# Exchanged halves of two weight matrices: VectorE copies between partition halves, or TensorE products with a permutation

## The chip, the cores and the metric

The kernel runs on one core of a Trainium2 chip. The metric is the device time of one execution in microseconds (us), the median of several executions. TensorE (PE in the profile; PEld is its weight load) multiplies, VectorE (DVE), ScalarE (ACT) and GpSimd (POOL) work on elements, SyncE (SP) issues transfers. Each engine works through its own queue in order and waits for others by semaphores.

## The reference

Attention over pooled queries, and then a multiplicative feed-forward block on its output:

```python
# q, k, v: (8 batches, 8 heads, 1152, 64)
q_pool = q.reshape(B, H, S // 2, 2, D).mean(axis=3)          # 576 queries
scores = scale * np.matmul(q_pool, k.transpose(0, 1, 3, 2))
attn = softmax(scores)
x = np.matmul(attn, v) -> (4608 tokens, 512)                 # heads side by side
a = x @ w1        # (512, 1024)
b = x @ w2        # (512, 1024)
h = a * b @ w3    # (1024, 1024)
out = h @ w_out   # (1024, 512)
```

Inputs and output are single precision; the kernel computes in half precision with single-precision sums.

## The kernel before

**Attention.** Two heads of one batch make a pair, one in partitions 0 to 63, the other in 64 to 127; there are 32 pairs, counted from 0. A pair's scores are 9 key blocks of 576 columns, cut through all pairs into 324 chunks of 512 columns. `scores` (L294) makes one chunk for both heads with products of half height, 64 rows each, so that the two heads' products run at the same time in two halves of the array (tile `psc`, two buffers). `expo` (L300) takes the exponential of both at once on ScalarE, into `er`. When a pair's chunks are done, two bursts (`attend`, L312 and L321, full-height products, tile `po`) multiply by the values; VectorE normalizes them (L340, L343, L354), and transposes on SP's queue (L348) put the result into `xT`, the left side of the feed-forward block.

**Keys and queries** of later pairs are turned by TensorE (`prep_pe`, tile `t`, L262; evicted by VectorE at L252 and L256), from pair 9 on by transposes on SP's queue (L166, L172).

**Feed-forward.** w3 and w_out are multiplied with each other once (`T16`; products `pT`, L477, evicted at L472, after transposes `w3t`, L465), so that each batch needs its gate products (`pg`, L514: x times w1 and x times w2, multiplied by VectorE at L497 and L506) and its output products (`pp`, L535). These products, too, are of half height: block `ft` of half h runs in rows 64h to 64h+63. Of a feature block m, the rows that half h needs lie in one partition half of the weights as they are loaded, and for the other m in the opposite one. So w1 and w2 are kept twice: `w1sb[:, 0]` as loaded, `w1sb[:, 1]` with partitions 0 to 63 and 64 to 127 exchanged. The gate products read `[(m + h) % 2]`:

```python
    nc.tensor.matmul(t, (w1sb, w2sb)[w][s, (m + h) % 2, m // 2, fs], x(s, m), ...)   # L514
```

**The exchange.** The weights are loaded in two column halves of 512 by POOL's queue (`load_ffn`, L376: w1sb, then w2sb, first half then second). `swap_halves` (L383) multiplies one block of 128 rows by 512 columns by a permutation matrix `swap` (L391) into a PSUM bank `sw`, and VectorE (L397) or, for one block of four, ScalarE (L394) writes it as half precision into `[:, 1]`. That is 4 blocks for each of 2 matrices and 2 column halves: 16 products, 12 evictions on VectorE, 4 on ScalarE. POOL builds `swap` from the identity with two copies (L638, L639).

**The order** of all this is made by a planner in the kernel while it records. It keeps a clock for each of TensorE's two halves (`clock`), one for VectorE (`vec`), the end of each exp (`exp_done`) and the PSUM banks in hand (`spare`), adds a booked cost for each block, and chooses what is recorded next: a burst when one is due, the next chunk when its exp buffer is free, otherwise one product of the waiting work (`step`: first keys, queries and w3 turns, then feed-forward). `swap_due` allows a permutation product when the planner's clock has passed 47 (first column half) or 57 (second) and enough banks are free; it is asked after each burst and wherever `step` finds nothing. The gate products of a column half are let in when its last exchange is done (`copied`). What is recorded is the fixed order on each engine; nothing is chosen while the kernel runs. A change of a booked cost therefore moves the order of everything after it, on all queues.

Of the kernel before, what the change touches and what calls it, by code (L numbers as in the profile page):

```python
# [8 lines left out]
FP16 = mybir.dt.float16  # L9
# [14 lines left out]
def kernel(  # L24
# [11 lines left out]
    nc = tc.nc  # L36
# [4 lines left out]
    NC = dm // 128  # L41
# [4 lines left out]
    T_SC, T_EXP, T_SEM, T_PV, LEAD = 0.219, 1.03, 0.25, (1.65, 1.3), 2.6  # L46
    SCALE = 0.5 * float(D) ** -0.5

    const = ctx.enter_context(tc.tile_pool(name="const", bufs=1))
# [14 lines left out]
    vts = [const.tile([128, 2, NJ, VW], FP16, name=f"vt{i}") for i in range(4)]  # L64

    ident = const.tile([128, 128], FP16)
    swap = const.tile([128, 128], FP16)
    seen = const.tile([1, 2], FP16)
    handed = const.tile([1, 1], FP32)

# [8 lines left out]
    clock = [0.0, 0.0]  # L79
    vec = 0.0  # L80
    exp_done = []
    spare = [(0.0, n) for n in range(4)]

    def vector(n, at):

        nonlocal vec
        vec = max(vec, at + T_SEM) + 0.16 + n / 960
        return vec

    def bank(pre, n, dt=FP32):  # L90
        if n >= 4:
            return psum.tile([128, 2, 512], FP32, tag="psc", bufs=2, name=pre)[:, 0, :]
        return psum.tile([128, 2048 // (4 if dt == FP32 else 2)], dt, tag=f"ff{n}", bufs=1,
                         name=pre)

    def take():
        return spare.pop(0)[1]

    def give(n, t):
        spare.append((t, n))  # L100
        spare.sort()
# [196 lines left out]
    def expo(c):  # L298
        r = (c * CH) % RING
        nc.scalar.activation(out=er[:, :, r:r + CH], in_=psc.pop(c), func=AF.Exp,  # L300
                             bias=0.0, scale=SCALE)

    def attend(P, u):

        n = take()
        po = bank("po", n)
        for j in range(NJ):
            for i in range(4):  # L310
                r = ((P * NJ + j) * SQ) % RING + 128 * i
                nc.tensor.matmul(  # L312
                    po[:, VW * i:VW * i + D + 1], er[:, u, r:r + 128],
                    vts[P % 4][:, u, j, 0:D + 1],
                    start=(j == 0 and i == 0), stop=(j == NJ - 1 and i == 3),
                    skip_group_check=True)
        if u == 0:
            for j in range(NJ):
                r = ((P * NJ + j) * SQ) % RING + 512
                for s in range(2):  # L320
                    nc.tensor.matmul(  # L321
                        po[64 * s:64 * s + 64, 4 * VW:4 * VW + D + 1], er[:, s, r:r + 64],
                        vts[P % 4][:, s, j, 0:D + 1], start=False, stop=(j == NJ - 1),
                        skip_group_check=True)
        at = max(clock[0], clock[1], exp_done[last_chunk(P)] + T_SEM) + T_PV[u]
        clock[:] = [at] * 2
        give(n, normalize(P, u, po, 5 - u, at))
        b, hp = divmod(P, 4)
        if u == 0 and b % 2 == 1:
            nc.sync.dma_start_transpose(  # L330
                out=xR[:, hp, b // 2].rearrange("p u r -> p (u r)"),
                in_=rems[:, hp].rearrange("p s d -> p (s d)"))
        if u == 0 and hp == 3:
            ended.append((b, [vec + (8.0 if b < 2 else 6.5)]))
# [29 lines left out]
    def load_w3(i):  # L364
        w3h.append(ffp.tile([128, 2, dff], FP16, tag="g", bufs=4, name="w3h"))
        nc.gpsimd.dma_start(
            out=w3h[i],
            in_=moe_w3.rearrange("(c p) f -> p c f", p=128)[:, 2 * i:2 * i + 2])
# [4 lines left out]
    def load_ffn(h):  # L373
        cols = slice(512 * h, 512 * h + 512)
        for dst, src in ((w1sb, moe_w1), (w2sb, moe_w2)):
            nc.gpsimd.dma_start(out=dst[:, 0, :, cols],  # L376
                                in_=src.rearrange("(c p) f -> p c f", p=128)[:, :, cols])
            swaps[h].extend((dst, c, cols) for c in range(NC))

    swaps = ([], [])  # L380
    copied = [[1e9], [1e9]]

    def swap_halves():  # L383

        half = 0 if swaps[0] else 1
        dst, c, cols = swaps[half].pop(0)
        n = take()
        t = bank("sw", n)  # L390
        nc.tensor.matmul(t, swap, dst[:, 0, c, cols], start=True, stop=True)  # L391
        clock[:] = [max(clock) + 0.22] * 2
        if c % 3 == 1:
            nc.scalar.copy(out=dst[:, 1, c, cols], in_=t)  # L394
            done = exp_done[-1] = max(exp_done[-1], clock[0] + T_SEM) + 0.6
        else:
            nc.vector.tensor_copy(out=dst[:, 1, c, cols], in_=t)  # L397
            done = vector(512, clock[0])
        give(n, done)
        if not swaps[half]:  # L400
            copied[half][0] = done + T_SEM

    def swap_due():
        half = 0 if swaps[0] else 1
        free = 3 if prep[0] or prep[1] else 2
        return bool(swaps[half]) and max(clock) > WEIGHTS[half] and len(spare) >= free and (
            spare[0][0] < min(clock))

    w3T = {}

# [26 lines left out]
    prep, ffn = ([], []), ([], [])  # L437
# [164 lines left out]
    def last_rows(places, lhsT):  # L602
# [24 lines left out]
        out=ident, in_=ident, compare_op=ALU.not_equal, fill=1.0,  # L627
# [7 lines left out]
    load_w3(1)  # L635
    load(3)
    load_w3(2)
    nc.gpsimd.tensor_copy(out=swap[:, 0:64], in_=ident[:, 64:128])  # L638
    nc.gpsimd.tensor_copy(out=swap[:, 64:128], in_=ident[:, 0:64])  # L639
    staged, prepped = 1, 1  # L640
    rest = prep_first()

# [18 lines left out]
    WEIGHTS = (47.0, 57.0)  # L661
# [5 lines left out]
    def due(c):  # L667


        if bursts and (c + 1) * CH > bursts[0][1] * PAIR + RING:  # L670
            return 1e9
        P = ((c + 1) * CH - 1) // PAIR
        return max(exp_done[c - 2] if c > 1 else 0.0, kq_done.get(P, 0.0))

    c = 0
    fresh = False
    while c < NCHUNK or bursts or ffn[0] or ffn[1]:
        h = 0 if clock[0] <= clock[1] else 1
        if bursts and (c > bursts[0][0] or c == NCHUNK) and spare and spare[0][0] < clock[h] and (
                fresh or c > bursts[0][0] + 1 or c == NCHUNK):  # L680
            attend(*bursts.pop(0)[1:])
            fresh = False
            while swap_due():
                swap_halves()
            continue
        if c >= NCHUNK or due(c) > clock[h]:
            fresh = False
            if c >= NCHUNK and not tail and not bursts:
                tail = True
                spare += [(max(clock), 4), (max(clock), 5)]  # L690
            keep = 1 if prep[0] or prep[1] or bursts and c > bursts[0][0] - 1 else 0
            if not step(h):
                if swap_due():
                    clock[:] = [max(clock) + 0.1] * 2
                    swap_halves()
                    clock[:] = [clock[0] + 0.1] * 2
                else:
                    clock[h] += 0.02
            while ended and not early and not prep[0] and not prep[1]:
                b, ready = ended.pop(0)  # L700
                add_batch(b, ready)
            continue
        at = c * CH / PAIR
        scores(c, h)
        fresh = True
        for i in range(2):
            clock[i] += T_SC
        expo(c)
        exp_done.append(max(exp_done[-1] if c else 0.0, max(clock) + T_SEM) + T_EXP)
        if c == 0:  # L710
            prep_rest(rest)
        if jobs:
            n, job = jobs.pop(0)
            job()
            vector(n, 0.0)
        if staged < NPE and at >= STAGE.get(
                staged, staged - (0.95 if staged < 4 else 1.3)):
            prep_stage(staged)
            staged += 1
        while events and at >= events[0][0]:  # L720
            _, n, act = events.pop(0)
            act(n)
        todo = prepped < NP and at >= PREP.get(prepped, prepped - (
            0.65 if prepped < 4 else 0.9 if prepped < NPE else 1.9))
        if todo and prepped >= NPE:
            prep_dma(prepped)
            prepped += 1
        elif todo and prepped < staged and prepped in kcs:
            prep_pe(prepped)
            prepped += 1  # L730
        elif early and c >= early[0][0] and len(w3T) < 4:
            w3_transpose(early.pop(0)[1])
        while turns and at >= turns[0][0]:
            turns.pop(0)[1]()
        c += 1
    for emit, store, _, _ in last[:-1]:
        n = take()
        t = bank("pp", n)
# [34 lines left out]
```

## Time and profile before

| | |
|---|---|
| time, median of 3 runs | 421.24 us (420.91 to 422.11) |
| span of the profiled execution, first to last instruction | 423.3 us |
| TensorE products by the permutation (L391) | 16, from 64.7 to 94.0 us |
| their evictions on VectorE (L397) | 12, 681 to 693 ns each, 8.2 us |
| their evictions on ScalarE (L394) | 4, 580 to 593 ns each, 2.4 us |
| first gate product (L514) | 76.0 us |
| POOL copies that build the permutation (L638, L639) | 2, at 21.5 and 21.7 us, 0.25 us each |
| loads of w1sb, issued / time to landing | 36.6 and 46.4 us / 15.9 us |
| loads of w2sb, issued / time to landing | 38.0 and 47.6 us / 17 us |
| granted TensorE clock, mean | 0.995 |

Of the profiled execution only its span is known, not its device time as the runs measure it. A busy share is a mean over the span; the chain of work that ended last is followed back from the last instruction and says for each piece of time which engine and line the end waited for. Matmuls are pipelined: a product's own duration (some 0.2 to 0.4 us) is longer than the spacing at which products follow each other, so that work is counted by the spacing or by its share of the chain. Lines named L are lines of the kernel before.

### The profile page before, as it was taken

Reading aid. Unit: us, or ns where it says so; the run is one execution under the profiler, and the core shown is the slowest. Engines: PE = TensorE matmul, PEld = TensorE weight load, DVE = VectorE, ACT = ScalarE, POOL = GpSimd, SP = SyncE. Lnnn points to the kernel's source line nnn. Section 1 sums busy time; section 2 is a strip of 40 time slices with the busy share of each in tenths; the row PEclk is TensorE's granted clock in tenths of the full one; section 3 lists DMA queues with packets and bytes.
Section 4 is the critical chain, followed back from the end, with each engine's and each line's share of the span. In section 5 each row is a group of like instructions: output and inputs, shape, how many; then the busy total and the mean of one; then the engine's idle time right before and its main releaser. Section 6 shows DMA issues by size and latency. Waiting matters only on the chain.

```text
span 423.3 us, 17431 instructions
## 1 busy us (share of the span) xinstructions
PE 403.7 (95%) x7666; PEld 318.0 (75%) x7666; DVE 218.9 (52%) x596; ACT 331.1 (78%) x382; POOL 191.2 (45%) x209
## 2 busy tenths in 40 slices
PE   3799999998999999999999899999999999999996
PEld 1366665777768887888788786788878887888993
DVE  2266656875435653565365663356446644542540
ACT  3968888887788888888888788889888888834432
POOL 8233345860566576555655556665569300000000
PEclk9999999999899999999999999999999999999999
DMA  8999999999699999999999999999996215102004
GB/s 120 206 207 202 186 205 204 189 161 121 110 154 206 152 141 153 196 144 121 192 170 132 139 134 132 190 185 150 137 170 141 42 35 133 43 19 101 4 11 141
DMA packets 94219, 59.02 MB, mean 139 GB/s; under 512 B 64832, under 2 KB 84544, under 8 KB 94144
## 3 DMA queue, kind: packets, MB, share of 16 engines
q0 software_dynamic: 26528, 33.56, 50.7%
q1 hardware_dynamic: 67456, 24.22, 35.1%
q8 instruction: 60, 0.98, 1.0%
q10 hardware_dynamic: 160, 0.13, 0.1%
q14 instruction: 15, 0.12, 0.1%
HBM read 67.11 MB, written 9.44 MB: 181 GB/s over the span
## 4 chain that ended last, share of the span: by engine, by line
PE 93%; ACT 3%; issue 2%; DMA 1%; DVE 0%; POOL 0%; DVEq 0%; ACTq 0%; POOLq 0%
PE pg L514 30%; PE psc L294 19%; PE po L312 18%; PE pp L535 15%; PE pT L477 4%; PE po L321 3%; ACT er L300 3%; PE t L262 1%; PE sw L391 1%; DMA kst<-in_k_dram 1%; PE w3t L465 0%; PE pp L608 0%; PE tb L195 0%; POOL qst L108 0%; ACT kc L207 0%
## 5 line engine op out<-in xcount | busy, mean ns | idle before, releaser
L300 ACT ACTIVATE er<-psc 128x1024 f16<-128x1024 f32 x324 | 308.8, 1030 | 52.0 <-PE psc L294 48.7
L294 PE MATMUL psc<-qT,kT 64*128 64x384 f16 (+7 forms) x1152 | 132.3, 291 | 4.6 <-ACT er L300 3.8
L514 PE MATMUL pg<-xT,w2sb 64*128 64x256 f16 x1024 | 131.3, 270 | 0.0
L514 PE MATMUL pg<-xT,w1sb 64*128 64x256 f16 x1024 | 130.7, 271 | 0.1
L514 PEld LDWEIGHTS <-w1sb 64*128 64x128 f16 x1280 | 97.9, 94 | 10.9 <-issue 2.7
L514 PEld LDWEIGHTS <-w2sb 64*128 64x128 f16 x1280 | 96.7, 94 | 6.2 <-issue 0.4
L535 PE MATMUL pp<-T,gT 64*128 64x512 f16 (+1 forms) x552 | 94.4, 376 | 0.0
L312 PEld LDWEIGHTS <-er 128*128 128x128 f16 x2304 | 74.5, 98 | 17.6 <-issue 15.0
L294 PEld LDWEIGHTS <-kT 64*128 64x128 f16 x1152 | 60.6, 95 | 32.5 <-issue 16.8
L312 PE MATMUL po<-vt,er 128*128 128x65 f16 x2304 | 82.4, 194 | 2.0 <-issue 1.8
L506 DVE TENSOR_TENSOR gT<-pg,asb 128x256 f16<-128x256 f32 (+1 forms) x160 | 66.3, 417 | 20.8 <-ACT asb L494 16.3
L497 DVE COPY asb<-pg 128x256 f32<-128x256 f32 (+1 forms) x119 | 48.0, 404 | 32.1 <-PE pg L514 30.5
L340 DVE RECIPROCAL rz<-po 128x4 f32<-128x4 f32 x64 | 12.1, 189 | 89.7 <-PE po L312 46.0
L143 POOL TENSOR_TENSOR qp<-qst 64x1152 f16<-64x1152 f16 x23 | 54.5, 2370 | 1.0
L535 PEld LDWEIGHTS <-gT 64*128 64x128 f16 (+1 forms) x552 | 41.3, 94 | 13.8 <-issue 0.4
L168 POOL COPY seen<-kT 1x1 f16<-1x1 f16 x19 | 3.4, 180 | 88.0 <-DMA kT<-kc 88.0
L152 POOL COPY vt<-vst 128x1152 f16<-128x1152 f16 x28 | 32.1, 1150 | 4.6 <-issue 3.9
L123 POOL DMA_DIRECT2D vst<-in_v_dram x32 | 23.3, 729 | 17.2 <-DMA kst<-in_k_dram 7.4
L116 POOL DMA_DIRECT2D kst<-in_k_dram x33 | 24.0, 729 | 11.7 <-issue 3.0
L343 DVE TENSOR_TENSOR xn<-po,rz 128x256 f16<-128x256 f32 x64 | 27.2, 424 | 2.2
L494 ACT COPY asb<-pg 128x256 f32<-128x256 f32 (+1 forms) x41 | 12.8, 332 | 19.4 <-PE pg L514 18.9
L161 POOL COPY kc<-kst 128x1152 f16<-128x1152 f16 x23 | 26.9, 1169 | 0.0
(62 smaller groups left out, 256.2 us busy)
## 6 DMA issues: line engine op xcount, KB each, us to landing
qst<-in_q_dram POOLq DMA_DIRECT2D x32, 288.0 KB, 6.0
vst<-in_v_dram POOLq DMA_DIRECT2D x32, 288.0 KB, 8.2
kst<-in_k_dram POOLq DMA_DIRECT2D x31, 288.0 KB, 5.4
out_dram<-osb SPq DMA_DIRECT2D x32, 256.0 KB, 3.2
w3h<-in_moe_w_dram POOLq DMA_DIRECT2D x4, 512.0 KB, 15.6
wosb<-in_moe_w_out_dram POOLq DMA_DIRECT2D x1, 1024.0 KB, 13.8
xT<-xn SPq DMA_TRANSPOSE x64, 5.8
w1sb<-in_moe_w_dram POOLq DMA_DIRECT2D x2, 512.0 KB, 15.9
```

The costliest lines, as they stand in the source:

```text
L116: nc.gpsimd.dma_start(out=kst[P][:, :, js[0]:js[1], :], in_=k[b, h0:h0 + 2].rearrange("u (p j) d -> p u j d", j=NJ)[:, :, js[0]:js[1], :])
L143: (eng or nc.vector).tensor_tensor(out=qps[pp][r].rearrange("p c u d -> p u c d"), in0=src[:, :, :, 0, :], in1=src[:, :, :, 1, :], op=ALU.add)
L152: (eng or nc.vector).tensor_copy(out=vts[P % 4][:, :, :, 0:D], in_=vst.pop(P))
L161: nc.gpsimd.tensor_copy(out=kc.rearrange("p j u d -> p u j d"), in_=kst.pop(P))
L294: nc.tensor.matmul(t[:, u, o:o + ln], kT[P][s, j, :], qv[s, f0:f0 + ln], start=True, stop=True)
L300: nc.scalar.activation(out=er[:, :, r:r + CH], in_=psc.pop(c), func=AF.Exp, bias=0.0, scale=SCALE)
L312: nc.tensor.matmul(po[:, VW * i:VW * i + D + 1], er[:, u, r:r + 128], vts[P % 4][:, u, j, 0:D + 1], start=(j == 0 and i == 0), stop=(j == ...
L343: nc.vector.tensor_tensor(out=xn, in0=acc[:, 0:4, 0:D], in1=rz[:, 0:4].to_broadcast([128, 4, D]), op=ALU.mult)
L497: nc.vector.tensor_copy(out=a, in_=t[:, 0:n])
L506: nc.vector.tensor_mul(out=g, in0=b, in1=a)
L514: nc.tensor.matmul(t[:, n * w:n * w + n], (w1sb, w2sb)[w][s, (m + h) % 2, m // 2, fs], x(s, m), start=start, stop=stop, skip_group_check=True)
L535: nc.tensor.matmul(t, gT[h][s, i, cs], T16[s, i, :], start=start, stop=stop, skip_group_check=True)
```

## The change

The permutation products, their evictions and the permutation are removed. `swap_halves` is now one VectorE copy from 64 partitions of `[:, 0]` to the other 64 partitions of `[:, 1]`, over all four row blocks of one column half: 64 x 4 x 512 elements, 8 copies in all (2 matrices, 2 directions, 2 column halves). The planner books 0.69 us on VectorE for each and nothing on TensorE or ScalarE, and takes no bank. One copy is recorded after a chunk of scores when no other VectorE job waits and the planner's clock has passed the same 47 or 57; the places where the old exchange was asked for are gone. ScalarE's line of exps has no other work in it before the last part of the kernel.

In the order of the instructions this puts the first four copies among pair 5's key and query evictions and the last four around pair 4's normalizations and pair 6's key and query evictions; the order is the same up to the first copy and differs in many places behind it. TensorE has 16 products and 16 weight loads fewer.

```diff
-    swap = const.tile([128, 128], FP16)
...
         for dst, src in ((w1sb, moe_w1), (w2sb, moe_w2)):
             nc.gpsimd.dma_start(out=dst[:, 0, :, cols],
                                 in_=src.rearrange("(c p) f -> p c f", p=128)[:, :, cols])
-            swaps[h].extend((dst, c, cols) for c in range(NC))
+            swaps[h].extend((dst, s, cols) for s in (0, 64))
...
-    def swap_halves():
-        half = 0 if swaps[0] else 1
-        dst, c, cols = swaps[half].pop(0)
-        n = take()
-        t = bank("sw", n)
-        nc.tensor.matmul(t, swap, dst[:, 0, c, cols], start=True, stop=True)
-        clock[:] = [max(clock) + 0.22] * 2
-        if c % 3 == 1:
-            nc.scalar.copy(out=dst[:, 1, c, cols], in_=t)
-            done = exp_done[-1] = max(exp_done[-1], clock[0] + T_SEM) + 0.6
-        else:
-            nc.vector.tensor_copy(out=dst[:, 1, c, cols], in_=t)
-            done = vector(512, clock[0])
-        give(n, done)
-        if not swaps[half]:
-            copied[half][0] = done + T_SEM
+    def swap_halves(half, dst, s, cols):
+        src = slice(64 - s, 128 - s)
+        nc.vector.tensor_copy(out=dst[s:s + 64, 1, :, cols], in_=dst[src, 0, :, cols])
+        vector(512, 0.0)
+        if not swaps[half]:
+            copied[half][0] = vec + T_SEM
 
-    def swap_due():
+    def swap_due(now):
         half = 0 if swaps[0] else 1
-        free = 3 if prep[0] or prep[1] else 2
-        return bool(swaps[half]) and max(clock) > WEIGHTS[half] and len(spare) >= free and (
-            spare[0][0] < min(clock))
+        if swaps[half] and now > WEIGHTS[half]:
+            swap_halves(half, *swaps[half].pop(0))
...
-    nc.gpsimd.tensor_copy(out=swap[:, 0:64], in_=ident[:, 64:128])
-    nc.gpsimd.tensor_copy(out=swap[:, 64:128], in_=ident[:, 0:64])
...
             attend(*bursts.pop(0)[1:])
             fresh = False
-            while swap_due():
-                swap_halves()
             continue
...
             if not step(h):
-                if swap_due():
-                    clock[:] = [max(clock) + 0.1] * 2
-                    swap_halves()
-                    clock[:] = [clock[0] + 0.1] * 2
-                else:
-                    clock[h] += 0.02
+                clock[h] += 0.02
...
             n, job = jobs.pop(0)
             job()
             vector(n, 0.0)
+        else:
+            swap_due(max(clock))
```

## The prediction

> **What bounds the kernel now.** I read the page first, for the busy shares and the chain of work that ended last.
>
> ```profile
> PE 403.7 (95%) x7666; PEld 318.0 (75%) x7666; DVE 218.9 (52%) x596; ACT 331.1 (78%) x382; POOL 191.2 (45%) x209
> ...
> PE 93%; ACT 3%; issue 2%; DMA 1%; DVE 0%; POOL 0%; DVEq 0%; ACTq 0%; POOLq 0%
> ```
>
> TensorE (PE) is on the chain for 93% of the span and VectorE (DVE) for 0%. So time taken off TensorE counts, unless it then waits for something else, and time put on VectorE counts only where TensorE must wait for it. Next I read the chain in the stretch from 60 to 77 us, where the exchange is made (start, us, what):
>
> ```profile
> by line: PE pT L477 26.1%; PE psc L294 25.2%; PE sw L391 18.8%; PE po L312 17.6%; PE po L321 4.8%; PE t L262 4.2%; PE pg L514 3.5%; issue 0.1%
> ...
> 64.80 0.32 PE sw L391
> 65.12 0.32 PE psc L294 x4
> ...
> 69.67 0.22 PE psc L294 x2
> 69.89 0.54 PE sw L391 x2
> 70.43 0.33 PE psc L294 x4
> ```
>
> The chain has no waits here: the permutation products (sw) lie on it whole, and the scores behind one take 0.32 us where others take 0.22. Third, ScalarE's timeline (start, us; the exps x4 stand in a row) shows how fast chunks of scores can follow each other:
>
> ```profile
> 56.72 3.77 ACT L300 ACTIVATE er<-psc 128x1024 f16<-128x1024 f32 x4 [0.25 <-PE psc L294]
> ```
>
> One exp lasts 1.02 us, four in a row 3.77, so they follow at (3.77 - 1.02) / 3 = 0.917 us. 324 of them need 297 us; the exps end near 371 us, so ScalarE has room.
>
> **The change, part by part.** *Removed from TensorE:* 16 products by the permutation. Eleven of them fill 18.8% of the 17 us above = 3.2 us, 0.29 each; 16 cost 4.7 us. About 0.3 us more goes with the slower scores behind them (0.10 each where no other full-height product is next to it, three places or so). Gross gain 5.0 us.
>
> *Given back.* TensorE's other work is the same but stands in another order: the first gate products (pg) come 210 score products into the order instead of 218, two chunks earlier, and the T products (pT) that the exchange used to alternate with are used up sooner. From the end of pair 3's second attend burst at 60.98 to the first gate product I added up the new order by the chain's pieces: ten chunks of scores 2.8, 27 T products 2.9, 27 transposes 0.8, two attend bursts 1.20 + 1.61: 9.3 us. Ten exps need 9.2, so there TensorE and ScalarE are even, and every unevenness is a wait. I walked both orders to the end this way: each product at its spacing in a run (T and output products 0.107 us, gate products 0.053, transposes 0.029, attend bursts 1.20 and 0.41, a permutation product 0.21), 0.10 at each change between half-height and full-height products, exps at least 0.917 apart, and a chunk's scores held until 0.25 us past the exp of two chunks before. TensorE waits 18.8 us in the old order (8 of them in the first 20 us) and 20.8 in the new one: 2.0 us are given back. At the same chunk the new order leads by 0.6 us (chunk 57), 1.6 (63), 2.3 (90), 2.9 (183) and 3.4 (240), and ends 3.0 earlier. With exps at 0.955 (what six at 96.75 us show), a hold of 0.15, or 0.05 to 0.15 per change, the end comes out 2.7 to 3.9 us earlier. I take 3.0.
>
> *Removed from ScalarE:* four evictions of 0.59 us, 2.4 us, in the walk. *Removed from VectorE:* 12 evictions, 8.2 us.
>
> *Added to VectorE:* 8 copies of 64 partitions x 2048 half-precision elements, SBUF to SBUF. No row copies between partition halves. The nearest are straight copies and evictions (count | busy us, mean ns | idle):
>
> ```profile
> L497 DVE COPY asb<-pg 128x256 f32<-128x256 f32 x103 | 43.5, 422 | 27.4 <-PE pg L514 25.8
> ...
> L397 DVE CAST w1sb<-sw 128x512 f16<-128x512 f32 x6 | 4.0, 687 | 0.6 <-PE sw L391 0.6
> ...
> L185 DVE COPY kc<-kst 128x1152 f16<-128x1152 f16 x6 | 2.7, 454 | 0.1
> ...
> L229 DVE COPY kc<-kst 128x768 f16<-128x768 f16 x1 | 0.3, 350 | 0.0
> ```
>
> The last two give 0.104 us per 384 elements, 0.271 ns each: 2048 elements cost 454 + 896 x 0.271 = 697 ns. The first two, out of PSUM, give 1.035 ns an element: at that pace a copy takes 687 + 1536 x 1.035 = 2.28 us. The low end is the first slope with no fixed part, 0.56 us. I take 0.70, because memory, type and kind of instruction are those of the L185 and L229 rows; only the partition offset is new. Eight cost 5.6 us, less than the 8.2 removed, but earlier and packed. VectorE (third of the engines' busy times) between 57 and 76 us:
>
> ```profile
> 57.00:76.00 19.00, 19.00 (x307) 11.14 (x304) 12.45 (x30) 16.53 (x19) 11.18 (x14) 1.00 1.21 203
> ```
>
> It is busy 12.45 of 19 us, with seven of the evictions (4.8 us) in it. With these out and eight copies in, it is 13.3: it fits. The tightest place is the first four copies, which stand in the order among pair 5's key and query evictions, right behind the normalization (xn) that ends at 56.97. Adding up 0.62 a copy (0.70 less the 0.08 by which neighbours overlap), two kT at 0.40, a T eviction 0.62, a handoff 0.12 and qT 0.38, qT is done at 61.4, against 58.7 now. Pair 5's scores begin in chunk 50, at 63.6 us: 2.2 us to spare. Behind qT the next normalization is some 0.5 us late, which delays a free PSUM bank and one transpose on SP, both with microseconds in hand (the chain shows no wait for either). If this cover is gone, every further microsecond lands on TensorE.
>
> *Waits.* The copies wait for the weights' DMAs. Where they stand, VectorE holds normalizations and evictions behind a copy that waits. POOL's own waits show the landings (last bracket: idle, who ended it):
>
> ```profile
> 52.70 0.60 POOL L108 DMA_DIRECT2D qst<-in_q_dram  x1 [2.69 <-DMA w1sb<-in_moe_w_dram]
> 55.38 0.72 POOL L123 DMA_DIRECT2D vst<-in_v_dram  x1 [2.09 <-DMA w2sb<-in_moe_w_dram]
> ...
> 65.36 0.60 POOL L108 DMA_DIRECT2D qst<-in_q_dram  x1 [1.73 <-DMA w2sb<-in_moe_w_dram]
> ```
>
> The first half is there by 55.4, its copies start at 57.0. In the second half w1sb was issued at 46.40 and takes 15.9, so 62.3, and its first copy comes near 64; w2sb is there by 65.3 and its copy stands behind pair 6's keys, near 68. No wait; 1.5 us to spare at the least. A weight landing 3 us late would hold VectorE for about 1.5.
>
> *POOL and SP:* two 0.25 us copies that built the permutation go; the load behind them waited for a DMA until 22.23 anyway: nothing. SP carries the same transposes and stores, with stores one or two places earlier or later; a store's issue takes 0.56 us (median), a transpose is 5.8 us on its way: at most half a microsecond of delay, under cover of the gate work that waits in line.
>
> *Against the change.* The row first: one straight VectorE copy (9.79 us, 0.45 long) ran while POOL issued a load at 9.98, and was no longer than the others (452 to 456 ns). [...]
>
> **The sum.** The profiled span is 423.3 us, 2.1 over the median 421.24 of the timed runs. Span: 423.3 - 5.0 + 2.0 = 420.3. The same 3.0 us off the median: 418.2. Own range by the walk 417.3 to 418.6, and 416.5 to 419.9 with half a pause (below) either way.
>
> **The rivals.**
>
> *Slow copies (slower than before).* If the crossing copy runs at the evictions' pace, it takes 2.28 us. The first four then end 4 x 1.58 = 6.3 us later; 2.2 are covered, so pair 5's scores stall about 4.1 us. The second four stand in what is left: VectorE's free 5.7 us in the stretch against 12.6 added in all, so about 2.8 more. 418.2 + 6.9 = 425.1; up to 427 if nothing is made up. It decides from about 0.70 + 2.2 / 4 = 1.25 us per copy, and the time is worse than before from 0.70 + (3.0 + 5.7) / 8 = 1.8. For it: no row of such a copy. Against it: same memories, type and instruction as the 454 ns row.
>
> *A pause moves.* TensorE stands still for "issue", for no semaphore, at 101.70, and at 105 its clock is halved (the chain's piece, then a row by time whose last columns are clock, DMA share, GB/s):
>
> ```profile
> 101.70 1.81 issue
> ```
>
> ```profile
> 105.00:106.00 1.00, 1.00 (x14) 0.73 (x10) 0.93 (x3) 1.00 (x2) 0.96 (x2) 0.50 0.00 0
> ```
>
> The clock is below 1 from 104.8 to 108.2, which costs 1.7 us: 3.5 in all. Others stand at 51.72 (0.61) and 240.60 (1.49). These places lie multiples of 256 TensorE instructions apart, and the page's row of the instruction queue has 60 packets of 16 KB for 15,332 instructions, which is one packet per 256: it looks like late code. The new program has 32 TensorE instructions fewer before all later places, so a packet's end falls elsewhere: without this pause 414.7, with one more 421.7. For it: two or three large pauses among 60 packets. Against: nothing shifts it one way.
>
> *TensorE thins out.* The gain is lost if the chunks from 61 to 71 us are paced by ScalarE and DVE answers rather than by products: 2.7 us more given back, 420.9, no change. For it: ten exps 9.2 against 9.3 us of products. Against: behind the first gate product a backlog lasts to the end, since 50 us of feed-forward work run after the last attend burst, and the walk already holds these waits. [...]
>
> **How the numbers follow.** Forecast (416.5 to 419.9) 0.52; slow copies 0.13; a pause fewer 0.08; a pause more or a thinned TensorE that ends within 0.3% 0.14; the same ending above that 0.13. 0.3% (1.26 us) is what a measurement of this kernel can tell from no change: 419.98 to 422.50. So faster 0.60, same 0.14, slower 0.26. The range leaves out about 1 in 10 at each end: 414.7 to 424.5.
>
> **What would show it.** sw is gone and w1sb<-w1sb copies stand at 0.65 to 0.75 us between 57 and 70; the first gate product starts at 70.5 to 72 us instead of 76.0; pair 5's scores show no wait for qT; the exps of the stretch follow at 0.92 to 1.0. Wrong if a copy lasts over 1.25 us, if VectorE waits for w1sb or w2sb landings, or if "issue" or a clock of 0.50 has grown or shrunk by over 1.5 us.

## The result, and the profile after

| | median | runs |
|---|---|---|
| before | 421.79 us (419.83 to 424.84) | 20 |
| changed | 423.99 us (421.03 to 428.20) | 20 |

The ratio changed / before is 1.0048, with an interval of 1.0026 to 1.0069: the change makes the kernel slower, by 2.2 us of the medians (the interval is 1.1 to 2.9 us). The runs of the changed kernel also spread more widely, over 7.2 us against 5.0.

One trap lies in the profiles themselves. The profiled execution of the changed kernel took 421.03 us, its fastest of 20, with a span of 419.0; so 2.0 us lie around the span. By the same 2.0 the profiled execution of before (span 423.3) took some 425.3 us, longer than each of its 20 timed runs. Laid side by side, the two profiles seem to show a gain of 4.3 us, and much of it is the pause and the halved clock between 101 and 108 us, which the changed kernel's profile doesn't have. Two profiles are two single executions; here only the medians carry the sign.

The page of the changed kernel (busy times, then the shares of the chain of work that ended last):

```profile
PE 400.5 (96%) x7650; PEld 315.6 (75%) x7650; DVE 218.9 (52%) x592; ACT 329.0 (79%) x378; POOL 190.8 (46%) x207
...
PE 91%; ACT 3%; DVE 2%; issue 2%; DMA 1%; POOL 0%; DVEq 0%; ACTq 0%; POOLq 0%
```

TensorE lost its 16 products. VectorE's busy time is the same to the tenth (218.9), though by the bookings it should have fallen by 8.2 - 5.6 = 2.6 us; and VectorE, which had no share of the chain, now has 2%. The groups of VectorE's instructions of one shape (count | busy us, mean ns | idle) show the copies:

```profile
L385 DVE COPY w2sb<-w2sb 64x2048 f16<-64x2048 f16 x4 | 3.6, 893 | 0.1
L385 DVE COPY w1sb<-w1sb 64x2048 f16<-64x2048 f16 x4 | 2.9, 736 | 0.1
L142 DVE TENSOR_TENSOR qp<-qst 64x1152 f16<-64x1152 f16 x8 | 8.0, 995 | 2.0 <-DMA qst<-in_q_dram 1.9
```

Six of the eight copies lasted 686 to 702 ns, one 880 and one 1494. The pooling of queries (L142, L143 before) has a mean of 995 ns where one lasts 0.74 to 0.76 us on both sides of the long one. VectorE's timeline by instruction shows the longest copy and the odd pooling (start, us):

```profile
60.93 1.49 DVE L385 COPY w2sb<-w2sb 64x2048 f16<-64x2048 f16 x1
...
73.64 2.75 DVE L142 TENSOR_TENSOR qp<-qst 64x1152 f16<-64x1152 f16 x1
```

and POOL's timeline of the same execution what ran beside them:

```profile
60.71 1.16 POOL L151 COPY vt<-vst 128x1152 f16<-128x1152 f16 x1
...
72.45 2.24 POOL L151 COPY vt<-vst 128x1152 f16<-128x1152 f16 x2
74.62 1.15 POOL L184 COPY kc<-kst 128x1152 f16<-128x1152 f16 x1
```

POOL's copy ends at 61.87, the VectorE copy that met it at 62.42. POOL's run of three ends at 75.77, the pooling at 76.39. So the VectorE instruction is not slowed in proportion: it lasts until POOL's run of copies is over and ends 0.55 and 0.62 us behind it, some 0.13 us less than it takes alone (0.69 and 0.75), as if it had begun only then. (The copy of 880 ns, at 68.65, stands beside a load that POOL issues at 68.33; the copies beside the loads issued at 70.03 and 71.73 lasted 0.70 and 0.69.) Three pieces of the chain of waits from 55 to 90 us show that the end waits for VectorE here:

```profile
68.65 0.88 DVE w1sb L385
...
73.64 2.75 DVE qp L142
76.42 0.44 DVE asb L483
```

VectorE is on this chain from 67.98 to 78.17 us, with three copies and the pooling; the copy of 1.49 us at 60.93 is not on it.

The other views that the prediction read hold no surprise. The stretch from 57 to 76 us (columns as before: busy times of PE, PEld, DVE, ACT, POOL, then clock, DMA share, GB/s):

```profile
57.00:76.00 19.00, 19.00 (x357) 13.42 (x353) 17.42 (x33) 16.34 (x18) 10.79 (x14) 1.00 1.21 202
```

VectorE is busy 17.42 of 19 us, where 13.3 were added up; 3.3 of the 4.1 between them are in the three long instructions: 0.8 and 0.2 in the copies, 2.3 in the pooling, which began only at 75.98 before. ScalarE's exps still follow at 0.917: five in a row take 4.69 us, (4.69 - 1.02) / 4.

POOL's waits for the weights (last bracket) are where they were, and no VectorE copy waits for them:

```profile
55.31 0.71 POOL L122 DMA_DIRECT2D vst<-in_v_dram  x1 [2.04 <-DMA w2sb<-in_moe_w_dram]
...
62.61 0.71 POOL L115 DMA_DIRECT2D kst<-in_k_dram  x1 [0.75 <-DVE w2sb L385]
65.23 0.60 POOL L107 DMA_DIRECT2D qst<-in_q_dram  x1 [1.90 <-DMA w2sb<-in_moe_w_dram]
```

The second of these lines is a load of keys that waits 0.75 us for a copy. Before, the same load waited 0.95 us for another VectorE instruction (`handed`, L434), so the copies cost nothing there.

### The profile page after: what moved, and what is told of

Same layout as the page of the kernel before. It is cut to its first block, busy times and chain, and to the rows that moved or that the text cites. A ratio compares the mean times of both kernels' runs of the same rounds, so it can differ in the third digit from the quotient of the medians.

```text
span 419.0 us, 17383 instructions
## 1 busy us (share of the span) xinstructions
PE 400.5 (96%) x7650; PEld 315.6 (75%) x7650; DVE 218.9 (52%) x592; ACT 329.0 (79%) x378; POOL 190.8 (46%) x207
## 4 chain that ended last, share of the span: by engine, by line
PE 91%; ACT 3%; DVE 2%; issue 2%; DMA 1%; POOL 0%; DVEq 0%; ACTq 0%; POOLq 0%
PE pg L500 29%; PE psc L293 19%; PE po L311 18%; PE pp L521 16%; PE pT L463 4%; PE po L320 3%; ACT er L299 3%; PE t L261 1%; DMA kst<-in_k_dram 1%; DVE qp L142 1%; PE w3t L451 0%; PE pp L594 0%; DVE w2sb L385 0%; DVE kT L255 0%; DVE w1sb L385 0%
## 5 line engine op out<-in xcount | busy, mean ns | idle before, releaser
L500 PE MATMUL pg<-xT,w2sb 64*128 64x256 f16 x1024 | 125.3, 269 | 0.8 <-issue 0.8
L500 PE MATMUL pg<-xT,w1sb 64*128 64x256 f16 x1024 | 124.6, 270 | 1.0 <-DVE gT L492 0.8
L500 PEld LDWEIGHTS <-w1sb 64*128 64x128 f16 x1280 | 96.3, 94 | 8.4 <-DVE gT L492 1.3
L293 PEld LDWEIGHTS <-kT 64*128 64x128 f16 x1152 | 61.8, 95 | 31.6 <-issue 15.8
L492 DVE TENSOR_TENSOR gT<-pg,asb 128x256 f16<-128x256 f32 (+1 forms) x160 | 66.2, 416 | 21.3 <-ACT asb L480 16.7
L142 POOL TENSOR_TENSOR qp<-qst 64x1152 f16<-64x1152 f16 x23 | 54.5, 2372 | 1.0
L480 ACT COPY asb<-pg 128x256 f32<-128x256 f32 (+1 forms) x41 | 12.8, 332 | 19.8 <-PE pg L500 19.3
```

What stands on the lines that cost most here:

```text
L142: (eng or nc.vector).tensor_tensor(out=qps[pp][r].rearrange("p c u d -> p u c d"), in0=src[:, :, :, 0, :], in1=src[:, :, :, 1, :], op=ALU.add)
L293: nc.tensor.matmul(t[:, u, o:o + ln], kT[P][s, j, :], qv[s, f0:f0 + ln], start=True, stop=True)
L492: nc.vector.tensor_mul(out=g, in0=b, in1=a)
L500: nc.tensor.matmul(t[:, n * w:n * w + n], (w1sb, w2sb)[w][s, (m + h) % 2, m // 2, fs], x(s, m), start=start, stop=stop, skip_group_check=True)
```

## The experiments

Two theories stood at the start. *Holds*: VectorE copies that meet POOL's copies wait them out, and TensorE waits for VectorE. *Order*: the new order of instructions costs time whatever makes the exchanged halves. A third came from the prediction, that late code (pauses for "issue" at multiples of 256 TensorE instructions; in the trace of before those at 51.72, 101.70 and 240.60 us stand 1789 and 5370 instructions apart, 7 x 256 less 3 and 21 x 256 less 6) falls in worse places. The expectations call the first theory P (port). No trace or run shows a port; what the runs can show of P is the holds. Kernels sent together share their runs of before, so each median is set against the before of its own group.

**The changed kernel again, without copies, and the old one without the exchange.** First the changed kernel unaltered (`after_again`) and the kernel before (`before_again`):

> The changed kernel again, unaltered, to see a profile of another execution beside its times. Theory P (port): VectorE's SBUF-to-SBUF work (the crossing copies, the query pooling) is held while POOL copies run, at 60.7 and 72.4 to 75.8 us; the profile shows one or more copies or poolings of 1 to 3 us in place of 0.7, and VectorE on the chain there; median 423 to 425. Theory C (late code): the holds are the same as in the profile at hand, and a longer span comes from pauses for issue and a halved clock elsewhere.

> The kernel before, unaltered: a profile of another execution. If the pause at 101.70 and the halved clock behind it belong to one execution in some, the span is 418 to 420.5 with no such pause; if they belong to the order, the span is again near 423.

Measured: 424.46 against 421.04, ratio 1.0066 (1.0030 to 1.0101); and one run of before at 421.89, span 420.0, in which nothing stands at 101.70. So the slowdown repeats, and the first profile of before was the odd one. The new profile of the changed kernel (span 426.5, one of its longest executions) has longer holds. VectorE:

```profile
59.56 1.84 DVE L385 COPY w2sb<-w2sb 64x2048 f16<-64x2048 f16 x1
...
71.04 3.95 DVE L385 COPY w2sb<-w2sb 64x2048 f16<-64x2048 f16 x1
```

and POOL beside it:

```profile
59.69 1.16 POOL L151 COPY vt<-vst 128x1152 f16<-128x1152 f16 x1
71.11 2.24 POOL L151 COPY vt<-vst 128x1152 f16<-128x1152 f16 x2
73.28 1.15 POOL L184 COPY kc<-kst 128x1152 f16<-128x1152 f16 x1
```

The copy at 71.04 starts 0.07 us before POOL's run, lasts through all three of its copies (end 74.43) and ends at 74.99. Behind it in VectorE's queue stands the eviction `qT`, and TensorE's waits in this profile name it (us in total, times, longest):

```profile
PE pg L500 <- DVE qT L251: 1.6, 1, 1.6
```

POOL's run stands right behind a load issue that waited for a load of keys to land (1.10 us in the first profile, 1.28 in this one). It starts at 72.45 us in the one and at 71.11 in the other; there it met the pooling and here a copy, which fits the wide spread.

Then the copies left out of the changed kernel (`after_no_copy`) and the products and evictions left out of the old one, in its old order (`before_no_exchange`). In both, the gate products read the unexchanged half, so half of the gate sums are of wrong rows:

```diff
-        nc.vector.tensor_copy(out=dst[s:s + 64, 1, :, cols], in_=dst[src, 0, :, cols])
...
-                ... (w1sb, w2sb)[w][s, (m + h) % 2, m // 2, fs],
+                ... (w1sb, w2sb)[w][s, 0, m // 2, fs],
```

```diff
-        t = bank("sw", n)
-        nc.tensor.matmul(t, swap, dst[:, 0, c, cols], start=True, stop=True)
...
-            nc.scalar.copy(out=dst[:, 1, c, cols], in_=t)
...
-            nc.vector.tensor_copy(out=dst[:, 1, c, cols], in_=t)
```

> The changed kernel with its order kept and the eight crossing copies left out (both halves of the gate products read the weights as loaded, so the exchange is not computed). P: without the copies VectorE reaches the poolings earlier and loses 5.6 us of work in the stretch: 418 to 420, clearly faster than before. C, or a worse order: the copies are not what costs, 422 to 424.

> The kernel before with its order kept and the 16 permutation products and their 16 evictions left out (the exchange is not computed). It prices the removed work by itself. By the chain it is 5.0 us: 416.5 to 418 against 421.8. If TensorE waits for the exps anyway in that stretch, 1 to 2.5 us: 419 to 421.

Measured: 422.28 (ratio 1.0024, 0.9999 to 1.0048) and 419.56 (0.9974, 0.9943 to 1.0004), against 421.04. Two things follow. The copies cost 2.2 us in the changed kernel, by medians whose intervals still overlap. And the exchange on TensorE, taken out of the old order without putting anything in its place, is worth 1.5 us (by the interval between 2.4 less and 0.2 more), not the 5.0 of the prediction's gross gain.

The held pooling doesn't need the copies. `after_no_copy` has it too, and on its chain:

```profile
73.04 2.77 DVE L142 TENSOR_TENSOR qp<-qst 64x1152 f16<-64x1152 f16 x1
```

`before_no_exchange` has one of 3.31 us, which is not on its chain. What the crossing copies bring is that they are held too, and stand in VectorE's queue beside it.

**POOL's copies taken away.** In the stretch of the exchange POOL's copies of values (pairs 4 to 8) and of keys (pairs 7 and 8) are made by VectorE at the same places of the order; TensorE's order is unchanged. In the changed kernel (`after_pool_free`) and as a control in the old one (`before_pool_free`):

```diff
-            copy_k(nc.gpsimd)
+            copy_k()
...
-            copy_v(P, nc.gpsimd)
+            copy_v(P)
```

> The changed kernel with TensorE's order kept; the value and key copies of pairs 4 to 8, which POOL makes between 60 and 95 us (1.15 us each), are made by VectorE at the same places (0.45 us each). Theory P (port): nothing on POOL holds VectorE any more; the crossing copies and the poolings all last 0.7 to 0.8 us, and the median falls by 1.5 to 3 us against the changed kernel (421 to 422.7 against 424.2). Theory C (late code, or the new order): the holds are not what costs, and with 3 us more work on VectorE the median is 424 or more.

> The same move of POOL's copies in the kernel before, as a control. P: no VectorE instruction was held there, so it gains nothing: within 1 us of before, rather slower, since VectorE has 3 us more. If it gains 1.5 us or more, the gain of the other kernel says nothing on the crossing copies.

Measured: 421.59 (0.9985, 0.9953 to 1.0017) and 422.42 (1.0011, 0.9986 to 1.0035), against 421.07. In the changed kernel VectorE has more work and the time falls; in the old kernel it does not. All eight copies now last 687 to 691 ns and all eight poolings 748 on average (two of the groups, columns as above):

```profile
L142 DVE TENSOR_TENSOR qp<-qst 64x1152 f16<-64x1152 f16 x8 | 6.0, 748 | 2.9 <-DMA qst<-in_q_dram 2.8
L385 DVE COPY w2sb<-w2sb 64x2048 f16<-64x2048 f16 x4 | 2.8, 689 | 0.1
```

From 73 to 80 us TensorE is busy 6.21 of 7 us in the changed kernel's first profile and all 7 here. First that one, then the one without POOL's copies (the number behind the comma is PE's busy time):

```profile
73.00:80.00 7.00, 6.21 (x110) 5.04 (x105) 6.46 (x12) 5.72 (x7) 6.33 (x8) 1.00 1.26 172
```

```profile
73.00:80.00 7.00, 7.00 (x148) 6.18 (x144) 5.97 (x17) 6.45 (x8) 2.94 (x5) 1.00 1.21 198
```

**Late code.** Sixteen idle transposes in chunks 2 to 5, 32 TensorE instructions, put the later instructions at their old numbers again, in the changed kernel (`after_padded`) and in the one without POOL's copies (`after_free_padded`):

```diff
+        if c in (2, 3, 4, 5):
+            pad = bank("pad", 3, FP16)
+            for n in range(4):
+                nc.tensor.transpose(pad[:, 128 * n:128 * n + 128], ident, ident)
```

> The changed kernel with 16 idle 128x128 transposes (32 TensorE instructions) in chunks 2 to 5, where TensorE waits 0.7 us a chunk for the exps, so that all later TensorE instructions have the number that they had before the change. C: the packet ends of TensorE's code fall where they fell, and the median falls by 1 us or more. P: within 0.7 us of the changed kernel.

> Both edits. P alone: as with POOL's copies moved, 421 to 422.7. P and C both: 420 to 421. Neither: 424 or more.

Measured: 423.13 (1.0037, 1.0008 to 1.0066) and 421.76 (1.0014, 0.9983 to 1.0045). Against 424.46 and 421.59 of the same kernels without the padding that is 1.3 less and 0.2 more, both inside the intervals. So the numbering is not shown to matter. An effect of some 1 us is not excluded either. With the transposes the clock is lower early on (in `after_padded` it is halved from 18.2 to 25.0 us, and its mean is 0.992, against 1.000 in both profiles of the changed kernel), but the first 40 chunks take no longer for it: 44.39 us from the first exp, against 44.80 in the changed kernel's first profile. The pair points the same way as the holds (423.13 with POOL's copies in place, 421.76 without), but its intervals overlap.

**Order against copies, with no holds.** POOL's copies moved in all four: the old order without the exchange (`no_exchange_free`), the new order without copies (`after_no_copy_free`; both leave the exchange out as above), the new order with each copy made twice (`after_free_twice`), and the old order with the new copies (`old_order_copies_free`). The last keeps the old kernel's bookings, and so its order, and records a crossing copy at every second place of a product:

```diff
-        t = bank("sw", n)
-        nc.tensor.matmul(t, swap, dst[:, 0, c, cols], start=True, stop=True)
+        if c % 2 == 0:
+            s = 32 * c
+            nc.vector.tensor_copy(out=dst[s:s + 64, 1, :, cols],
+                                  in_=dst[64 - s:128 - s, 0, :, cols])
```

> The kernel before in its order, without the exchange (not computed), and with POOL's value and key copies of pairs 4 to 8 on VectorE. With POOL's copies in place this was 419.6 against 421.0, and one pooling was held for 3.3 us. Theory P: the hold ate part of the gain: 416.5 to 418. Theory S: TensorE then waits for the exps in the stretch and the removed products are worth only 1.5 to 2 us there: 419 to 421, as the move costs before itself 1 us.

> The changed kernel in its order, without the crossing copies (not computed), and with POOL's copies moved. It prices the new order by itself, against the run above. If the new order is as good as the old: within 1 us of it. If it costs what it seemed to with POOL's copies in place (422.3 against 419.6): 2 to 3 us more.

> The changed kernel with POOL's copies moved and each crossing copy made twice: 5.6 us more of VectorE in the stretch, with nothing on POOL to hold it. By the slack of the prediction (2.2 us at the first four copies, which now get 2.5 more) TensorE stalls by 0.5 to 1.5 us: 422 to 423.5 against 421.6. If VectorE had no slack: 424 to 427.

> The exchange by the eight crossing copies, but recorded in the order of the kernel before (every second place of a permutation product records one copy, with the old bookings), and POOL's copies moved. All of the output is computed. If the new order costs 1.5 us or more: 419 to 420.5, faster than before. If the copies cost it by themselves: 421 or more, as with the new order (421.6).

Measured, against 420.57: 419.51 (0.9974, 0.9947 to 1.0002), 422.06 (1.0031, 0.9995 to 1.0067), 427.21 (1.0162, 1.0122 to 1.0202) and 419.69 (0.9971, 0.9944 to 0.9998). The new order alone is 2.5 us longer than the old one. The copies, where nothing holds them, cost nothing that can be measured in either order (421.59, from the group before, against 422.06; 419.69 against 419.51). Without copies the held pooling costs nothing that can be measured either: 419.51 against 419.56 with the hold in the old order, where 416.5 to 418 was expected if the hold cost time, and 422.06 against 422.28 in the new one. Twice the copies, 5.6 us more on VectorE, end 5.6 us later than one set (421.59 in the group before; by the two ratios it is more): past the one set there is no slack.

**The old order with the copies, POOL's copies in place and moved.** `old_order_copies` has the edit above alone; `old_order_copies_free2` is the last kernel again:

> The crossing copies in the order of the kernel before, with POOL's copies of pairs 4 to 8 left on POOL. Theory P: the copies at 72 to 76 us and the pooling there are held until POOL's run of copies ends, 2 to 3.5 us on VectorE; TensorE loses 1 to 2.5 us of it: 420.7 to 422.2 against 419.7. If the old order has cover enough for the holds: 419.5 to 420.3.

> A second sample of the crossing copies in the old order with POOL's copies moved: 419 to 420.5, ratio 0.995 to 0.999. If the first sample was luck: 420.5 to 421.5.

Measured, against 421.8: 425.61 (1.0088, 1.0052 to 1.0123) and 419.34 (0.9955, 0.9925 to 0.9985). The first came out well above what was expected of it: in the old order the copies fall right beside POOL's runs, and the holds cost 6 us. In the profile some 1.7 of these are TensorE's clock, halved for 3.4 us behind the wait (0.50 from 81.2 to 84.6 us; an estimate, 3.4 x 0.5). The chain of `old_order_copies` from 70 to 85 us shows VectorE on it without a break from 71.42 to 80.86, and then TensorE's burst:

```profile
72.24 2.42 DVE w2sb L392
...
76.14 3.28 DVE qp L143
...
80.16 0.70 DVE T L472
...
80.91 1.94 PE po L312 x36
```

TensorE's waits in the same execution name the eviction that came last in this queue (us in total, times, longest):

```profile
PE po L312 <- DVE T L472: 4.3, 1, 4.3
```

With POOL's copies moved (`old_order_copies_free2`), the same copies last 687 to 691 ns each, two of them 1.41 us here, and VectorE's timeline at the same place reads:

```profile
71.98 1.41 DVE L392 COPY w2sb<-w2sb 64x2048 f16<-64x2048 f16 x2
...
74.63 0.76 DVE L143 TENSOR_TENSOR qp<-qst 64x1152 f16<-64x1152 f16 x1
```

This kernel computes the whole output and is faster than both: 0.29% and 0.45% below before in two groups of runs.

The medians, by order and by what is in the kernel (us):

| | POOL's copies in place | moved to VectorE |
|---|---|---|
| old order, products (before) | 420.57 to 421.8 | 422.42 |
| old order, no exchange | 419.56 | 419.51 |
| old order, crossing copies | 425.61 | 419.69, 419.34 |
| new order, no exchange | 422.28 | 422.06 |
| new order, crossing copies (changed) | 423.99, 424.46 | 421.59 |

## Why the prediction was wrong

The forecast was 418.2 us, faster; 423.99 lies near the upper end of its range, on the other side of before. Two steps failed: the sum has nothing for the copies' meetings with POOL's, and TensorE's other work was taken to last as long in the new order as in the old one.

**The copies beside POOL's.** The sum has no term for them. That was wrong in the number of meetings, in the length of one, and in who is held. Copies met POOL's near 60 and near 71 us, the pooling met them near 74; one meeting lasts as long as POOL's whole run, up to 4.09 us for a 0.69 us copy (3.95 above, 4.09 in `after_padded`); and the two-input pooling is held like the copies (2.75 us above, 3.28 in `old_order_copies`, 0.75 alone). The row that stands under *Against the change*, a VectorE copy beside a load issue, was of the wrong kind: a load issue is no POOL copy, and no row of before had a straight VectorE copy beside a POOL copy. What the meetings cost is the interaction in the table. In the new order the copies cost 2.2 us with POOL's copies in place and nothing with them moved; in the old order 6 us and nothing.

Why VectorE is held is not shown. Which of the two starts first does not settle it: by the profile of `after_again` both held copies started before POOL's (59.56 against 59.69 us, 71.04 against 71.11), and yet they ended 0.55 and 0.56 us behind POOL's run. The run of three at 71.11 has no gap (two copies end at 73.35, the third starts at 73.28), and VectorE's copy did not end between them. Where POOL's next instruction started 0.07 us behind the end of the one before (89.60 and 89.67), VectorE's copy ended at 90.16, 0.56 us behind the first, and POOL's second, a copy, lasted 1.50 us in place of 1.15. In `old_order_copies`, VectorE's line first, then POOL's two:

```profile
89.13 1.03 DVE L392 COPY w2sb<-w2sb 64x2048 f16<-64x2048 f16 x1
```

```profile
87.25 2.35 POOL L143 TENSOR_TENSOR qp<-qst 64x1152 f16<-64x1152 f16 x1
89.67 1.50 POOL L152 COPY vt<-vst 128x1152 f16<-128x1152 f16 x1
```

Before the change nothing met this way: in the whole profile of before not one of VectorE's straight copies and poolings in SBUF overlaps one of POOL's copies or poolings, so that profile could show neither the hold nor its absence. VectorE's work beside POOL's run at 72.06 to 75.38 was evictions out of PSUM, 0.68 us each as always, and the pooling came at 75.98, just behind the run.

**The gross gain.** "16 cost 4.7 us", and 0.3 for the scores behind them, was read off the chain: 18.8% of the 17 us. As TensorE's work it was about right: TensorE is busy 402.5 us in `before_again` and 402.0 in `before_pool_free`, and 396.9 and 398.2 in the same two kernels without the exchange. The time fell by less: 1.5 us with POOL's copies in place (419.56 against 421.04), and with them moved 2.9 by the medians of two groups (419.51 against 422.42) or 1.6 by their ratios. Here the share of the chain is what the products occupied, not what their absence brings. Part of it comes back as waits for exps, here in `no_exchange_free` (us in total, times, longest; it was 3.8 in 9 waits):

```profile
PE psc L294 <- ACT er L300: 5.1, 13, 0.7
```

The starts of the exps show where something is left of the gain. Between chunk 48 and chunk 60, where 11 of the 16 products lay, the three profiles of the old order with products take 14.37 us each and the five without 12.23: 2.14 us of the 3.5 that 11 products and their neighbours were booked at. From chunk 60 to 84, where the other five lay, two undisturbed profiles take 26.89 and 27.22 us with them and 27.05 and 27.28 without: nothing.

**The new order.** The walk gave back 2.0 us as waits, for the removal and the new order together. That size was about right: TensorE's idle time, its span less its busy time, is 17.5 us in `before_again` and 19.6 in `after_no_copy`, and with POOL's copies moved 18.9 and 21.3. But the new order also costs busy time. Against the old order without the exchange it takes 2.7 us more (422.28 against 419.56), with POOL's copies moved 2.5 (422.06 against 419.51), and most of this is not waiting, as the first lines of two pages show, `before_no_exchange` and then `after_no_copy`:

```profile
PE 396.9 (95%) x7650; PEld 316.4 (76%) x7650; DVE 214.7 (51%) x584; ACT 329.0 (79%) x378; POOL 191.3 (46%) x209
```

```profile
PE 400.6 (95%) x7650; PEld 314.7 (75%) x7650; DVE 212.6 (51%) x584; ACT 329.2 (78%) x378; POOL 190.9 (45%) x207
```

The same 7650 products keep TensorE busy 3.7 us longer, while it is idle 20.3 and 19.6 us. With POOL's copies moved they keep it busy 2.5 us longer (398.2 and 400.7), and it is idle 19.3 and 21.3 us, a pause for "issue" of 1.8 us among them. So the step that failed here is "TensorE's other work is the same but stands in another order": the walk took it to last as long in both. In place of 5.0 less, TensorE is busy 1.9 and 1.3 us less in the new order without copies than before. Which products run at a wider spacing, and why, is not shown. The new order without copies and holds is then 1.2 to 1.5 us longer than before by the medians, though both intervals still reach down to no change. The starts of the exps in the two profiles of each order that have neither exchange nor copies (us; POOL's copies in place, moved):

```
chunks            old order       new order
40 to 48          8.87   8.87     9.44   9.44
48 to 60         12.23  12.23    12.19  12.19
60 to 84         27.05  27.28    27.53  28.00
84 to 132        51.91  51.90    51.97  51.98
132 to 156       26.12  26.12    26.69  26.73
156 to 300      159.93 159.30   160.39 161.62
behind the last  53.40  53.39    53.86  53.83
```

A longer stretch is not a loss by itself, because the orders place different work in it: from chunk 40 to 48 the new order has 177 products where the old one has 171, from 132 to 156 it has 519 and 503, and behind the start of the last exp 877 and 869. In chunks 132 to 156 all eight profiles of the old order take 26.12 us, and those of the new one 26.16 to 27.68, with pauses for "issue" in some (1.41 us at 173.18 in `after_pool_free`). Why they fall there in the new order stays open; the padding didn't settle it.

**What held.** The copy's price: 697 ns predicted, 686 to 691 measured in `after_pool_free`, where nothing holds it; the rival with a copy at the evictions' pace named a time of 425.1 that is near the result, and the right place (VectorE late, TensorE waiting), for a wrong cause. The 2.2 us to spare: eight copies of 0.69 cost nothing without holds, but double that costs all that is added. The weights' landings: no copy waited. POOL and SP: POOL's own time did not matter (moving its copies gains nothing where no crossing copy stands), but that its copies stand beside VectorE's did. The first gate product came at 72.7 us where 70.5 to 72 was named.

**The rivals.** *A pause moves* is what made the two first profiles look like a gain of 4.3 us; the timed runs can't tell pauses from other costs, so what they are worth in the new order stays open. *TensorE thins out* is not what happened in the changed kernel: TensorE waits 3.6 and 3.8 us for exps in its two profiles, in 9 waits each, as before. In the old order without the exchange these waits rise to 5.5 and 5.1. Where TensorE is thin in the first profile of before, from 10 to 20 us (busy 6.79 of 10 us), its clock is not known: the record of the clock starts at 22.9 us. A score product of 512 columns lasts 604 ns from 15 to 20 us and 375 from 40 to 50 (medians of four).

The sum, by the medians of the first group: -1.5 for the removed work, +2.7 for the order (422.28 against 419.56), +2.2 for the held copies, in all 3.4, which is 424.46 - 421.04. It must close, since each term is the difference between two neighbours of one row of medians; the 20 runs gave 2.2 for the whole. Of the 6.4 us between this and the forecast's -3.0, the holds are 2.2, and the removed work and the order together 4.2.

## What to carry to other kernels

Before moving work to VectorE as copies inside SBUF, list GpSimd's copies in that stretch. Here a VectorE copy or two-input operation with all its operands in SBUF that met a run of them ended 0.55 to 0.63 us behind the run (a copy lasted 1.49 to 4.09 us in place of 0.69), while evictions out of PSUM kept their 0.68 us. What mattered was who queued behind it: the held pooling alone cost nothing that could be measured (422.28 against 422.06 us, 419.56 against 419.51). Take work off an engine in an experiment before believing its share of the chain; here 5.0 us on the chain were worth some 1 to 3. Where an order changes, compare TensorE's busy time as well as its waits: here the same 7650 products took 3.7 us longer (396.9 and 400.6). Where a planner makes the order, keep the old order in one experiment and change the work alone: it separates the edit from the reshuffle, and here it also gave the fastest kernel.

## What the runs showed of the hardware

- A straight VectorE copy in SBUF (0.69 us alone) lasted 1.49, 1.84, 2.42 and 3.95 us beside runs of one to three GpSimd copies, and the two-input pooling (0.75 alone) 2.75 and 3.28; each ended 0.55 to 0.63 us after GpSimd's run. GpSimd's copies beside these kept their 1.15 to 1.16 us. In one other meeting, at 89.13 us in `old_order_copies`, VectorE's copy (1.03 us) began beside a GpSimd pooling and ended 0.56 us behind it, and GpSimd's copy, begun 0.07 us behind that pooling, lasted 1.50 us. Evictions out of PSUM beside GpSimd's copies were not held (0.68 to 0.69 us for 512 columns). Beside a load that GpSimd issues, VectorE's copies were mostly as long as alone (0.70 and 0.69 us at 70.42 and 71.51 in the first profile of the changed kernel); some were 0.2 us longer (0.88 for 0.69 at 68.65 there, 0.64 for 0.46 at 59.76 in `after_pool_free`).
- A copy of 64 partitions into the other 64 costs what one in place would by the slope of the straight copies of before (697 ns): 686 to 691 ns for 2048 half-precision elements.
- In two executions (mean granted clock 0.995 in both) TensorE's clock was halved for 3.4 us shortly after TensorE had stood still: in the first profile of before from 104.8 us, after the pause of 1.81 us at 101.70, and in `old_order_copies` from 81.2 us, after the wait of 4.3 us that ended at 80.91. Not every pause was followed by it: the clock stayed at 1.00 behind one of 1.49 us at 240.60 in the same profile of before, and the mean clock is 1.000 in `before_again`, which has one of 1.51 us at 237.55, and in `after_no_copy_free`, which has one of 1.8 us. A row of `old_order_copies` (columns as above, the clock is the third last):

```profile
83.00:84.00 1.00, 1.00 (x18) 0.82 (x16) 0.49 (x2) 0.51 (x1) 1.00 (x3) 0.50 1.17 206
```

- TensorE's pauses for "issue" vary from one execution to the next. `after_pool_free` has the changed kernel's TensorE order, and its chain has these pieces (start, us, what):

```profile
173.18 1.41 issue
...
285.13 1.09 issue
```

where the changed kernel's first profile has its largest pause at 241.63 (1.26 us) and none near these two.
